# Delta-rule attention and two MoE layers on one core: the first MoE's weight words move to ScalarE's queue, with new priorities for keys and inverses

## The chip, the core and the metric

The kernel runs on one core of a Trainium2 chip. The metric is the device time of one execution in microseconds; the time given is the median of several executions. The core's engines are TensorE (PE in the rows), VectorE (DVE), ScalarE (ACT), GpSimd (POOL) and SyncE (SP). SP only issues DMAs here; ScalarE computes and issues some DMAs as well, in the order in which its instructions stand. A queue of DMAs is named after the engine that issues them (SPq, ACTq).

## The reference

Three layers follow one another; inputs are random, and the arithmetic of the kernel is in float32, with operands split in a high and a low part where TensorE works on them.

```python
# 1. delta-rule attention: 4 x 8 sequences, 768 steps, head size 48
k_n = k / (norm(k) + 1e-6)
for t in range(768):
    y[t] = q[t] @ state
    v_old = k_n[t] @ state
    state = state + beta[t] * outer(k_n[t], v[t] - v_old)
# 2. first MoE: x = y as (3072, 384)
h = x @ w_in                      # w_in (384, 2048), stored as float64
x = (h * sigmoid(h)) @ w_out      # w_out (2048, 384), stored as float64
# 3. second MoE: 8 experts, gate normalised by rows and columns 8 times
out = sum(P[:, e:e+1] * (relu(x @ w1[e]) @ w2[e]) for e in range(8))
```

## The kernel before

**Attention in chunks.** The 768 steps are cut into 12 chunks of 64, which the program calls steps s, and the 32 sequences into two groups bp = 0, 1. For each chunk the recurrence turns into matrix products once a 64 x 64 triangular system is inverted. For two chunks at a time, `tri(j)` inverts the diagonal 32 x 32 blocks of chunks 2j and 2j+1 of all sequences on VectorE: a start (line 538), 62 dependent operations, one column after the other (lines 546 and 548), and an end (line 561) that gives `tu`. ScalarE copies `tu` to `nu` in another order (line 564), SP writes both to memory (`rd`, line 569; `td`, line 578) and loads them back in the layout in which TensorE needs them (`rt`, line 588; `td11`, lines 593 and 596). `merge(s)` makes the off-diagonal block with TensorE (`z`, line 607; `r`, line 620), and the products `c`, `d`, `y`, `s`, `t` follow.

What an inverse needs are the key Grams of its two chunks. For chunks 2 and up, `keys(s, prio)` loads the keys (`ke`, line 354, by SP), makes two Gram tiles for each group on TensorE (`gkq`, lines 398 and 399), copies them from PSUM on ScalarE (line 414), and stores them by SP (`nd`, line 408; `gd`, line 404). There are 40 such tiles. `units(j)` reads `nd` back as `nu` (line 432). The roots that scale an inverse are taken on ScalarE for the first two (line 474) and on GpSimd for the others.

**The first MoE** runs while attention goes on: six batches b of 512 tokens, each ready when two chunks are done. For each of 16 blocks f of the hidden dimension TensorE makes `h` (nine products of 128 x 512, line 733) and `x2p` (nine, line 774). Between the two ScalarE takes the Sigmoid (line 739), VectorE multiplies (line 743), ScalarE rounds to the high part (line 747) and GpSimd makes the low part (line 751).

**Its weights** arrive as 64-bit words. `weight(kind, f, m)` loads one or two blocks (`wr`, line 861; 768 KB for two) and converts them: ScalarE takes the absolute value of the high words (line 865), VectorE runs seven operations (lines 886 to 897), ScalarE writes the high part (line 883). There are 20 such conversions, 12 of them pairs; n counts single blocks, 0 to 31. The words of pair n take the place of an earlier one, so their load waits until the absolute value of an earlier block is taken (`free`).

**The second MoE** starts at about 760 us in the profile, and takes the rest of the time.

**The order** is written by a list scheduler, the class `Order`. Each operation is added with an engine, a cost, what it depends on and a priority; the scheduler keeps a clock of each engine, and of the operations that could start first it takes the one with the highest priority. The result is a fixed order on each engine. SP alone is modelled as a queue of DMAs, with 8 in flight; a DMA on ScalarE is an operation of ScalarE with its issue as cost, and what waits for it is given a latency by hand. The names in the order below carry the step, the group and a running number: `gkq4_1_0` is the Gram 0 of step 4, group 1.

Of the kernel before, what the change touches and what calls it, by code (L numbers as in the profile page):

```python
# [12 lines left out]
I32 = mybir.dt.int32  # L13
# [188 lines left out]
def kernel(  # L202
# [14 lines left out]
    nc = tc.nc  # L217
# [10 lines left out]
    def f32(ap):  # L228
        return ap.bitcast(F32)
# [3 lines left out]
    def place(p, i=None, shape=(3072,), dtype=F32R, name=None):  # L233

        tag = f"w{p}" if i is None else f"w{p}_{i}"
        return persist.tile([128, *shape], dtype, tag=tag, name=name or tag)
# [55 lines left out]
    op = sc.add  # L292
    T = {}
    O = {}
# [8 lines left out]
    for i in range(4):  # L303
# [3 lines left out]
        out=nident, in0=tmpu[:, 0:128], in1=tmpu[:, 0:128], op=ALU.add), [(x, 0.13)], prio=40)  # L307
# [20 lines left out]
    def load_part(s, bp, part, prio):  # L328

        t = kplace(s, bp)  # L330
        a, b = slice(64, 112), slice(0, 48)
        after = [(x, -1.0) for x in O["nl", 0]] + [O["z", 2 * s + bp]] if part else []
        if s and not part:

            return [(op("ACT", 0.45, adma(t(a, 0), kq[s, bp, 0, :, 0]), prio=prio), 2.3),
                    (op("ACT", 0.45, adma(t(b, 0), kq[s, bp, 1, :, 0]), prio=prio), 2.3)]
        return [op("SP", 0.27, dma(t(a, part), kq[s, bp, 0, :, part]), after, prio=prio),
                op("SP", 0.27, dma(t(b, 2 * part), kq[s, bp, 1, :, part]), after, prio=prio)]
# [10 lines left out]
    def load_k(s, bp, prio):  # L349
        def go(ab):  # L350
            if ab == 0:
                T["ke", s, bp] = two.tile([128, 2, H, CH], F32, tag="ke", name=f"ke{s}_{bp}")
            o = 64 * (1 - ab)
            nc.sync.dma_start(out=T["ke", s, bp][o:o + 48], in_=kq[s, bp, ab])
        x = op("SP", 0.5, lambda: go(0), [(y, -1.0) for y in O["nl", 0]], prio=prio, take=["ke"])
        return [x, op("SP", 0.5, lambda: go(1), [(x, -9.0)], prio=prio)]
# [483 lines left out]
    def weight(kind, f, m):  # L840

        src, n = (w_out if kind else w_in), 4 * (f // 2) + 2 * kind + f % 2
        key = ("wr", n)
# [6 lines left out]
        p, i = n // 4, n % 4  # L850

        def ld():
            if p < NP - 2:
                if i == 0:
                    T["pw", p] = place(p + 1, shape=(4 * DM, 2), dtype=I32, name=f"wr{p}")
                T[key] = T["pw", p][:, DM * i:DM * (i + m)]
            elif n < 2 * NF - 1:
                T[key] = place(NP - 1, i + (p == NP - 1), (DM, 2), I32, f"wr{n}")
            else:
                T[key] = moe.tile([128, DM, 2], I32, tag="wx", bufs=1, name=f"wr{n}")  # L860
            nc.sync.dma_start(out=T[key], in_=src[:, f:f + m].bitcast(I32).rearrange("p f (c w) -> p (f c) w", w=2))

        def absolute():
            T["wt", n] = moe.tile([128, 2 * DM], F32, tag="stg", bufs=3, name=f"wt{n}")
# [32 lines left out]
            (1, lambda: v.scalar_tensor_tensor(out=part(1), in0=view(lw().bitcast(U32)), scalar=2.0 ** -43, in1=view(f32(hw())),  # L897
                                               op0=ALU.mult, op1=ALU.mult)),
        ]
        free = [O["wabs", n - 4 + j] for j in range(m)] if n >= 4 else []  # L900
        if n >= 4:
            free = free + [(x, -1.0) for x in O["nl", 0]]
        if 2 * NF - 4 <= n < 2 * NF - 1:
            free = free + [O["wlo", n - 3]]
        a = op("SP", 1.09 * m, ld, free, prio=-9 if n >= 4 else 9.2)
        first = op("ACT", 0.1 + 0.35 * m, absolute, [a] + ([O["wabs", n - 1]] if m == 1 and n else []), prio=-4, take=["stg"])

        if p == NP - 1:
            before = [O["wlo", n - 1 if i else n - 4]]
# [5 lines left out]
        for k, (two_, fn) in enumerate(ops):  # L915
            c = 0.09 + 0.47 * m if two_ else 0.13 + 0.22 * m
# [10 lines left out]
    def keys(s, prio):  # L927
        for bp in range(2):
            O["ke", s, bp] = load_k(s, bp, prio) if s >= 2 else load_part(s, bp, 0, prio)
            (gram_kq if s >= 2 else gram_k)(s, bp)  # L930
# [11 lines left out]
    for s in range(2):  # L942
# [5 lines left out]
        out=wgr[:, :, 1], in0=wgs, in1=f32(wgr)[:, :, 0], op=ALU.subtract), [x], prio=0)  # L948
    for p in range(NP):
        for kind in range(2):  # L950
            for f in range(2 * p, 2 * p + 2, 2 if p < NP - 2 else 1):
                weight(kind, f, 2 if p < NP - 2 else 1)
# [4 lines left out]
    for s in range(NSTEP):  # L957
        if s % 2 == 0 and s + 2 < NSTEP:
            if s:
                keys(s + 2, 6)  # L960
                keys(s + 3, 6)
            units(s // 2 + 1)
            tri(s // 2 + 1, 1.5 if s else 1.6)
        O["rtl", s], O["gll", s], O["tdl", s] = rt_load(s)
        merge(s)
        for bp in range(2):
            if s:
                state_read(s, bp)
            update(s, bp)
            output(s, bp)  # L970
            turn(s, bp)
            k = 2 * s + bp
            k = k + 4 if k < 3 else k + 3 if k > 3 else 2 * NSTEP
            if k < 2 * NSTEP:
                O.setdefault(("ld", k // 2), {})[k % 2] = load(k // 2, k % 2, -2.5)
                mask_q(k // 2, k % 2)
        if s + 2 < NSTEP:
            O["kv", s + 2] = load_kv(s + 2, -3.5)
            norms(s + 2)
        if s % 2:  # L980
            for f in range(NF):
                moe_h(s // 2, f)
                moe_o(s // 2, f)
# [458 lines left out]
```

## Time and profile before

| | us |
|---|---|
| median of 3 executions | 2282.77 (2282.16 to 2282.86) |
| profiled execution | 2280.6 |
| its span, first to last instruction | 2278.8 |
| TensorE busy | 2187.4 (96%) |
| VectorE busy | 1768.9 (78%) |
| GpSimd busy | 1552.9 (68%) |
| ScalarE busy | 1018.5 (45%) |
| mean granted TensorE clock | 0.973 of full speed |

The profile comes from one execution. The chain of work that ended last runs 61% of the span on TensorE, 15% on VectorE, 11% on GpSimd and 5% through DMAs. These are shares over the whole span; the stages differ, and the rows further down are read by stage.

### The profile page before, as it was taken

Reading aid. Unit: us, or ns where it says so; the run is one execution under the profiler, and the core shown is the slowest. Engines: PE = TensorE matmul, PEld = TensorE weight load, DVE = VectorE, ACT = ScalarE, POOL = GpSimd, SP = SyncE. Lnnn points to the kernel's source line nnn. Section 1 sums busy time; section 2 is a strip of 40 time slices with the busy share of each in tenths; the row PEclk is TensorE's granted clock in tenths of the full one; section 3 lists DMA queues with packets and bytes.
Section 4 is the critical chain, followed back from the end, with each engine's and each line's share of the span. In section 5 each row is a group of like instructions: output and inputs, shape, how many; then the busy total and the mean of one; then the engine's idle time right before and its main releaser. Section 6 shows DMA issues by size and latency. Waiting matters only on the chain.

```text
span 2278.8 us, 40177 instructions
## 1 busy us (share of the span) xinstructions
PE 2187.4 (96%) x15662; PEld 1918.5 (84%) x15662; DVE 1768.9 (78%) x2999; ACT 1018.5 (45%) x1766; POOL 1552.9 (68%) x1387
## 2 busy tenths in 40 slices
PE   7789998999999899999999999989999999999999
PEld 7677776788787789999898999978999999999998
DVE  6788776623825688888888888897888888888887
ACT  2344333333344446454444544446444454545453
POOL 0225165344428678888788888877878888888884
PEclk8689999999999999999999999999999999999999
DMA  8764534432120200101111111111111111110101
GB/s 244 183 144 129 144 76 91 104 75 66 36 65 34 84 28 28 42 29 38 33 35 35 35 35 30 41 46 39 36 35 36 35 35 36 35 35 28 43 28 49
DMA packets 127421, 136.76 MB, mean 60 GB/s; under 512 B 83392, under 2 KB 91328, under 8 KB 127232
## 3 DMA queue, kind: packets, MB, share of 16 engines
q1 hardware_dynamic: 124864, 133.55, 21.6%
q8 instruction: 123, 2.02, 0.4%
q10 hardware_dynamic: 2368, 0.66, 0.2%
q14 instruction: 66, 0.54, 0.1%
HBM read 108.47 MB, written 25.69 MB: 59 GB/s over the span
## 4 chain that ended last, share of the span: by engine, by line
PE 61%; DVE 15%; POOL 11%; DMA 5%; issue 3%; ACT 2%; SPq 2%; POOLq 0%; DVEq 0%; ACTq 0%
PE o L1291 29%; PE p L1204 23%; PE x2p L774 3%; DVE s L1014 3%; POOL room L1014 2%; DVE tu L546 2%; PE h L733 2%; DVE tmpu L548 2%; POOL wa L1014 2%; POOL wraw L1014 2%; POOL g L751 1%; POOL h L1014 1%; DMA ke<-in_kq 1%; DVE sg L743 1%; POOL du L524 1%
## 5 line engine op out<-in xcount | busy, mean ns | idle before, releaser
L1204 PE MATMUL p<-room,wa 128*128 128x512 f32 x2880 | 738.0, 397 | 5.5 <-DVE s L1014 5.5
L1204 PEld LDWEIGHTS p<-room,wa 128*128 128x128 f32 x2880 | 537.7, 189 | 104.2 <-issue 5.9
L1291 PE MATMUL o<-wb,room 128*128 128x384 f32 x2784 | 603.9, 339 | 2.9 <-POOL room L1014 0.9
L1014 DVE TENSOR_TENSOR s<-s,p 128x512 f32<-128x512 f32 x704 | 476.2, 684 | 161.4 <-ACT s L1218 77.5
L1291 PEld LDWEIGHTS o<-wb,room 128*128 128x128 f32 x2784 | 499.8, 189 | 25.5 <-DVE acc L1307 6.5
L1014 POOL TENSOR_TENSOR room<-s,room 128x512 fp32r<-128x512 f32 x232 | 317.7, 1370 | 235.3 <-ACT s L1237 134.3
L1307 DVE SCALAR_TENSOR_TENSOR acc<-o,pr,acc 128x384 f32<-128x384 f32 x708 | 418.6, 612 | 34.2 <-PE o L1291 32.7
L1291 PE MATMUL o<-wb,h 128*128 128x384 f32 x1824 | 420.0, 338 | 3.1 <-DVE acc L1014 1.6
L1291 PEld LDWEIGHTS o<-wb,h 128*128 128x128 f32 x1824 | 329.6, 188 | 22.7 <-issue 2.2
L1014 POOL TENSOR_TENSOR wa<-wraw,wa 128x640 fp32r<-128x640 f32 x189 | 323.5, 1724 | 1.7 <-ACT wa L1107 1.7
L1235 ACT ACTIVATE room<-s 128x512 fp32r<-128x512 f32 x232 | 145.6, 628 | 387.8 <-DVE s L1014 387.8
L751 POOL TENSOR_TENSOR g<-sg,g 128x512 fp32r<-128x512 f32 x96 | 131.1, 1367 | 239.6 <-ACT g L747 239.2
L1014 POOL TENSOR_TENSOR wraw<-wraw 128x256 f32<-128x256 f32 x378 | 274.8, 748 | 13.9 <-DMA wraw<-in_w 4.2
L1237 ACT ACTIVATE s<-s 128x512 f32<-128x512 f32 x384 | 243.1, 633 | 12.2
L774 PE MATMUL x2p<-g,w 128*128 128x512 f32 x864 | 229.7, 409 | 18.5 <-POOL g L751 14.1
L1107 ACT ACTIVATE wa<-wraw 128x640 fp32r<-128x640 f32 x189 | 138.4, 732 | 234.8 <-POOL wraw L1014 218.3
L733 PE MATMUL h<-x,w 128*128 128x512 f32 x864 | 224.1, 409 | 3.1 <-ACT x L709 0.9
L1014 DVE TENSOR_TENSOR s<-p,s 128x512 f32<-128x512 f32 x320 | 219.1, 685 | 6.0 <-PE p L1204 1.8
L1014 POOL TENSOR_TENSOR h<-s,h 128x512 fp32r<-128x512 f32 x152 | 210.9, 1388 | 9.5 <-ACT s L1237 9.5
L774 PEld LDWEIGHTS x2p<-g,w 128*128 128x128 f32 x864 | 159.7, 192 | 63.3 <-POOL g L751 22.8
L1014 DVE TENSOR_TENSOR s<-s,s 128x512 f32<-128x512 f32 x192 | 210.8, 1098 | 2.3
L733 PEld LDWEIGHTS h<-x,w 128*128 128x128 f32 x864 | 164.7, 195 | 40.1 <-DVE sg L743 1.4
(177 smaller groups left out, 2246.6 us busy)
## 6 DMA issues: line engine op xcount, KB each, us to landing
wraw<-in_w SPq DMA_DIRECT2D x126, 384.0 KB, 3.0
kv<-in_kv SPq DMA_DIRECT2D x12, 768.0 KB, 4.9
ke<-in_kq SPq DMA_DIRECT2D x40, 192.0 KB, 3.6
kqp<-in_kq SPq DMA_DIRECT2D x40, 192.0 KB, 4.1
nd<-ke SPq DMA_DIRECT2D x20, 256.0 KB, 2.1
gd<-ke SPq DMA_DIRECT2D x20, 256.0 KB, 3.7
kqp<-gd SPq DMA_DIRECT2D x40, 128.0 KB, 4.0
wr<-in_w_in SPq DMA_DIRECT2D x6, 768.0 KB, 6.5
```

What stands on the lines that cost most here:

```text
L546: nc.vector.tensor_tensor(out=tu[:, a:b, 0:k], in0=tu[:, a:b, 0:k], in1=tv, op=ALU.add)
L548: nc.vector.tensor_tensor(out=tv, in0=nu[:, a:b, t:k].to_broadcast([128, b - a, k]), in1=tu[:, t:k, 0:k].to_broadcast([128, b - a, k]), op ...
L733: nc.tensor.matmul(out=ps.rearrange("p (s t) -> p s t", s=2), lhsT=w[:, k, wl], rhs=X1[:, at, k, xl], start=n == 0, stop=n == 8)
L751: nc.gpsimd.tensor_tensor(out=g[:, 1], in0=T["sg", b, f], in1=f32(g)[:, 0], op=ALU.subtract)
L774: nc.tensor.matmul(out=T["x2p", b][j], lhsT=w[:, wl, 128 * j:128 * j + 128], rhs=g[:, gl], start=f == 0 and n == 0, stop=f == NF - 1 and n ...
L1014: e.tensor_tensor(out=out, in0=in0, in1=in1, op=o)
L1107: nc.scalar.activation(P2[key][:, :, 0], R(3 + 5 * g, 8 + 5 * g), AF.Copy)
L1204: nc.tensor.matmul(out=ps, lhsT=w[:, i, wl], rhs=x[:, xl], start=k == 0, stop=k == 2)
L1235: nc.scalar.activation(P2[key][:, 0], buf(x), AF.Relu)
L1237: op2("ACT", 0.52, lambda: nc.scalar.activation(buf(x), buf(x), AF.Relu), writes=[("s", n, x)], prio=PR_H)
L1291: nc.tensor.matmul(out=ps, lhsT=h[:, hl, 128 * i:128 * i + 128], rhs=w[:, wl], start=c == 0, stop=c == 5)
L1307: op2("DVE", 0.53, lambda A=A, pk=pk, t=t: nc.vector.scalar_tensor_tensor(out=A(), in0=P2[pk], scalar=P2["pr"][:, t, e:e + 1], in1=A(), op ...
```

## The change

It moves the load of the words of the first MoE's weights from SP to ScalarE (line 861). In the scheduler's terms that operation is now one of ScalarE with 0.45 us, and the absolute value waits 2.5 + 2.5 m us behind it. The load of block n waits for the absolute value of block n − 8 instead of n − 4. The priority of these loads is −3 instead of −9. The keys of steps 4 and up get −12 instead of 6, and the inverses from the third on 1.2 instead of 1.5.

```diff
-            nc.sync.dma_start(out=T[key], in_=src[:, f:f + m].bitcast(I32).rearrange("p f (c w) -> p (f c) w", w=2))
+            nc.scalar.dma_start(out=T[key], in_=src[:, f:f + m].bitcast(I32).rearrange("p f (c w) -> p (f c) w", w=2))
...
-        free = [O["wabs", n - 4 + j] for j in range(m)] if n >= 4 else []
+        free = [O["wabs", n - 8 + j] for j in range(m)] if n >= 8 else []
...
-        a = op("SP", 1.09 * m, ld, free, prio=-9 if n >= 4 else 9.2)
-        first = op("ACT", 0.1 + 0.35 * m, absolute, [a] + ([O["wabs", n - 1]] if m == 1 and n else []), prio=-4, take=["stg"])
+        a = op("ACT", 0.45, ld, free, prio=-3 if n >= 4 else 9.2)
+        first = op("ACT", 0.1 + 0.35 * m, absolute, [(a, 2.5 + 2.5 * m)] + ([O["wabs", n - 1]] if m == 1 and n else []), prio=-4, take=["stg"])
...
             if s:
-                keys(s + 2, 6)
-                keys(s + 3, 6)
+                keys(s + 2, -12)
+                keys(s + 3, -12)
             units(s // 2 + 1)
-            tri(s // 2 + 1, 1.5 if s else 1.6)
+            tri(s // 2 + 1, 1.2 if s else 1.6)
```

The order that the scheduler writes differs from there on in many places. Three of them follow.

ScalarE ahead of the square root of the first inverse (line 474), before the change; what stands in brackets is what the instruction waits for, DMAHW and a number being one of the eight semaphores that DMAs share in turn:

```order
L883 ACTIVATE w_229<-wt_198 128x6x128 [waits DVE_49]
L432 DMA nu<-nd_224 16x32x32 [waits DMAHW5_49,DMAHW0_49]
L432 DMA nu<-nd_224 16x32x32 [waits DMAHW2_49]
L883 ACTIVATE w_229<-wt_221 128x2x384 [waits DVE_49]
L474 ACTIVATE du<-rta 128x32 [waits DVE_49]
```

The same place with the change:

```order
L432 DMA nu<-nd_220 16x32x32 [waits DMAHW5_49,DMAHW0_49]
L432 DMA nu<-nd_220 16x32x32 [waits DMAHW2_49]
L883 ACTIVATE w_276<-wt_231 128x6x128 [waits DVE_49]
L861 DMA wr_289<-in_w_in 128x1536 [waits DMAHW4_49]
L861 DMA wr_289<-in_w_out 128x1536 [waits DMAHW7_49]
L861 DMA wr_304<-in_w_in 128x1536 [waits DMAHW1_49]
L861 DMA wr_304<-in_w_out 128x1536 [waits DMAHW4_49]
L474 ACTIVATE du<-rta 128x32 [waits DVE_49]
```

Four loads of words now stand between the loads of `nu` and the root, and the last of them waits for semaphore 4, which the first of them was given.

ScalarE around the copy of the first inverse (line 564), before:

```order
L414 ACTIVATE ke3_0_472<-gkq3_0_1_597 128x512
L414 ACTIVATE ke3_0_472<-gkq3_0_0_621 128x512
L865 ACTIVATE wt8_668<-wr2_572 128x768
L414 ACTIVATE ke3_1_556<-gkq3_1_1_646 128x512
L414 ACTIVATE ke3_1_556<-gkq3_1_0_674 128x512
L564 ACTIVATE nu_94<-tu_95 128x32x32
L414 ACTIVATE ke4_0_723<-gkq4_0_1_778 128x512
```

and with the change:

```order
L414 ACTIVATE ke3_0_466<-gkq3_0_1_529 128x512
L414 ACTIVATE ke3_0_466<-gkq3_0_0_552 128x512
L414 ACTIVATE ke3_1_522<-gkq3_1_1_577 128x512
L414 ACTIVATE ke3_1_522<-gkq3_1_0_604 128x512
L414 ACTIVATE ke4_0_635<-gkq4_0_1_662 128x512
L414 ACTIVATE ke4_0_635<-gkq4_0_0_691 128x512
L414 ACTIVATE ke4_1_683<-gkq4_1_1_721 128x512
L564 ACTIVATE nu_94<-tu_95 128x32x32
L414 ACTIVATE ke4_1_683<-gkq4_1_0_751 128x512
```

Three Gram copies of step 4 (`ke4_0`, `ke4_1`) that came behind the copy to `nu` now come ahead of it, and the absolute values of line 865 are gone from this stretch.

ScalarE where Grams of steps 10 and 11 are copied: before, they stand in the middle of the third batch of the MoE (`sg2_12` is the Sigmoid of batch 2, block 12), behind the `z` of step 8:

```order
L414 ACTIVATE ke10_1_3340<-gkq10_1_1_5449 128x512
L739 ACTIVATE sg2_12_5511<-h2_12_5484 128x512
L747 ACTIVATE g2_12_5523<-sg2_12_5511 128x512
L414 ACTIVATE ke10_1_3340<-gkq10_1_0_5494 128x512
L739 ACTIVATE sg2_13_5555<-h2_13_5528 128x512
L747 ACTIVATE g2_13_5571<-sg2_13_5555 128x512
L414 ACTIVATE ke11_0_3587<-gkq11_0_1_5538 128x512
L739 ACTIVATE sg2_14_5607<-h2_14_5578 128x512
L747 ACTIVATE g2_14_5619<-sg2_14_5607 128x512
L414 ACTIVATE ke11_0_3587<-gkq11_0_0_5590 128x512
```

With the change, the last of the 40 Gram copies stands in the second batch, right ahead of the copy of `z` of step 6 (`zt6`):

```order
L564 ACTIVATE nu_94<-tu_95 128x32x32
L678 ACTIVATE y5_1_4278<-y5_1_4238 128x384
L739 ACTIVATE sg1_12_4315<-h1_12_4281 128x512
L747 ACTIVATE g1_12_4334<-sg1_12_4315 128x512
L739 ACTIVATE sg1_13_4353<-h1_13_4321 128x512
L747 ACTIVATE g1_13_4359<-sg1_13_4353 128x512
L739 ACTIVATE sg1_14_4379<-h1_14_4341 128x512
L414 ACTIVATE ke11_1_3137<-gkq11_1_0_4361 128x512
L613 ACTIVATE zt6_4431<-z6_4385 32x512 x2
```

So the Gram tiles that were spread to the third batch and beyond lie ahead of step 6.

## Rows read from the trace of the kernel before

**Rows 1.** Windows: length, busy time of each engine, clock, DMA share, GB/s.

```profile
0.00:126.00 126.00, 96.25 (x1712) 90.64 (x1712) 92.62 (x269) 40.43 (x71) 18.53 (x27) 0.74 0.81 209
126.00:256.00 130.00, 117.03 (x1510) 91.46 (x1510) 113.98 (x215) 57.49 (x99) 48.41 (x42) 0.93 0.56 135
...
760.00:2279.00 1519.00, 1496.89 (x7502) 1353.39 (x7502) 1299.46 (x2035) 738.85 (x1258) 1240.98 (x1090) 0.99 0.12 38
```

**Rows 2.** Tile `wr` (words): ns min/median/max, starts; last, landing.

```profile
L889 DVE SCALAR_TENSOR_TENSOR wt<-wr,wt x20: 551/951/2014, 12.3 to 250.6; 128x768 int32<-128x768 int32 x12, 128x384 int32<-128x384 int32 x8
L891 DVE TENSOR_SCALAR wr<-wr x20: 350/544/1181, 13.7 to 251.1; 128x768 int32<-128x768 int32 x12, 128x384 int32<-128x384 int32 x8
L893 DVE SCALAR_TENSOR_TENSOR wr<-wr x20: 546/952/1074, 14.3 to 251.7; 128x768 int32<-128x768 int32 x12, 128x384 int32<-128x384 int32 x8
L895 DVE TENSOR_SCALAR wr<-wt x20: 349/552/565, 15.3 to 252.3; 128x768 int32<-128x768 int32 x12, 128x384 int32<-128x384 int32 x8
L897 DVE SCALAR_TENSOR_TENSOR w<-wr x20: 540/946/1464, 15.9 to 253.3; 128x768 fp32r<-128x768 uint32 x12, 128x384 fp32r<-128x384 uint32 x8
...
DMA to landing us min/median/max: 3.3/5.5/10.9
```

**Rows 3.** SP's timeline, 20 to 66 us: start, duration, line, operation.

```profile
33.74 0.45 SPq L861 DMA_DIRECT2D wr<-in_w_in  x1
...
35.58 7.29 SPq L354 DMA_DIRECT2D ke<-in_kq  x4
...
54.65 5.71 SPq L354 DMA_DIRECT2D ke<-in_kq  x4
...
61.95 0.50 SPq L569 DMA_DIRECT2D rd<-nu  x1
```

**Rows 4.** The chain of waits to 60 us: issue, us to landing.

```profile
4.03 6.08 DMA wr<-in_w_in
...
16.48 3.36 DMA nd<-gneg
...
35.94 11.47 DMA ke<-in_kq
```

**Rows 5.** ScalarE's timeline to 130 us; in brackets idle time and its releaser.

```profile
24.55 0.23 ACT L474 ACTIVATE du<-rta 128x32 f32<-128x32 f32 x1 [2.83 <-DVE rta L472]
...
54.06 1.95 ACT L564 ACTIVATE nu<-tu 128x1024 f32<-128x1024 f32 x1
```

**Rows 6.** VectorE: ends of inverses 1 and 3, two multiplies of the MoE.

```profile
48.83 1.23 DVE L561 TENSOR_TENSOR tu<-tu,du 128x1024 f32<-128x1024 f32 x1
...
172.15 0.69 DVE L743 TENSOR_TENSOR sg<-h,sg 128x512 f32<-128x512 f32 x1 [5.18 <-ACT sg L739]
...
241.18 0.69 DVE L743 TENSOR_TENSOR sg<-h,sg 128x512 f32<-128x512 f32 x1 [4.07 <-ACT sg L739]
...
273.37 1.23 DVE L561 TENSOR_TENSOR tu<-tu,du 128x1024 f32<-128x1024 f32 x1
```

**Rows 7.** TensorE's timeline, 125 to 438 us: rows with waits.

```profile
125.80 0.51 PE L733 MATMUL h<-x,w 128*128 128x512 f32 x1 [0.93 <-ACT x L709]
...
224.61 2.14 PE L774 MATMUL x2p<-g,w 128*128 128x512 f32 x8 [1.20 <-DVE w L897]
...
234.67 0.29 PE L398 MATMUL gkq<-ke 48*64 48x64 f32 x2 [2.39 <-DMA ke<-in_kq]
...
358.67 1.72 PE L607 MATMUL z<-rt,td 32*32 32x32 f32 x64 [4.52 <-DMA rt<-rd]
...
437.38 0.22 PE L607 MATMUL z<-rt,td 32*32 32x32 f32 x2 [1.03 <-DMA rt<-rd]
```

**Rows 8.** Windows, tile `gkq` (key Grams) alone, 438 to 625 us.

```profile
438.00:625.00 187.00, 6.89 (x192) 6.06 (x192) 3.50 (x6) 1.00 0.27 67
```

**Rows 9.** Windows, 590 to 626 us, all engines.

```profile
590.00:626.00 36.00, 31.04 (x186) 23.21 (x185) 26.44 (x53) 10.29 (x15) 9.59 (x7) 1.00 0.19 38
```

**Rows 10.** Windows, 20 to 50 us, all engines.

```profile
20.00:50.00 30.00, 22.55 (x290) 21.79 (x290) 25.44 (x131) 6.58 (x11) 0.00 (x0) 0.81 1.00 277
```

## The prediction, made before the changed kernel was run

> **What bounds the kernel now.** I read the windows view first, by stage. After 760 us TensorE is busy 1496.89 of 1519 us [rows 1]: the second MoE is bound by TensorE's work, and the change moves nothing there. What can move is the time at which that stage begins. Before it TensorE is idle for 126 − 96.25 = 29.75 us up to the first product of the first MoE (`h`, at 125.80) and for 13 us in the 130 us after that [rows 1, 7].
>
> The second view was what releases the first stage. On the chain of waits the words of the first weights take 6.08 us from issue to landing, and a load of keys issued at 35.94 takes 11.47 us [rows 4]. SP's own rows say why: words issued at 33.74 (and more of them right behind) stand in the same queue ahead of these keys, and SP's group of four key loads lasts 7.29 us, a later one 5.71 us; only behind that can SP issue `rd`, at 61.95 [rows 3]. `rd` is the inverse on its way to memory. The inverse itself ended at 48.83 + 1.23 = 50.06 on VectorE [rows 6], and its copy on ScalarE ran at 54.06 for 1.95 [rows 5].
>
> The third view was TensorE's waits later on: 4.52 us for `z` at 358.67 and 1.03 at 437.38, both for `rt`, that is, for an inverse [rows 7]. So from 125 to 440 us the chain of inverses (`tri`) on VectorE sets the end, and work that TensorE could do beside it only fills waits.
>
> "Measurable" means here more than 0.2%, 4.6 us. The sum is made against the profiled execution (2280.6 us; 2278.8 of span, 1.8 around it) and laid on the median, 2282.77, 2.2 above it.
>
> **The change part by part.** *Words to ScalarE's queue, first stage.* SP loses 20 issues of words, 0.45 us for the one shown [rows 3], and the words that lie in its queue ahead of keys; keys come sooner. Against that, ScalarE now issues words in order with its computing. Ahead of the square root of the first inverse stand four loads of words, and the last waits for the semaphore that the first of them was given, so the root cannot start before that load has landed. Ahead of this group ScalarE has loads of `nu` that need `nd`, and `nd` landed at 16.48 + 3.36 = 19.8 [rows 4]; 6.08 us later [rows 4] is 25.9, against 24.55 for the root before [rows 5]: the root comes some 1.4 us late, unless `nd` comes sooner with no words ahead of it. Next, the copy of the inverse (`nu`, line 564) now stands behind three more Gram copies, which need keys of step 4; before, they came behind it. I expect the copy at 59 to 61 instead of 54.06. But SP issued `rd` at 61.95 only, so most of that delay has cover: SP, which was blocked until then, is free now. If that cover is gone, the delay counts in full. Term: **+1.0**. Bounds: below, `rd` could go right behind the inverse and its copy, 50.06 + 1.95 = 52.0, not 61.95: −9.9. Above, words land after 10.9 us at worst [rows 2]; twice 10.9 − 6.1 is +9.6. I take a value near the middle since both waits are visible and both have cover.
>
> *Eight tiles ahead, and the inverses against the conversion.* Of the conversion five instructions fewer stand ahead of the first multiply of the MoE on VectorE (one each of lines 889, 891, 893, 895, 897): medians 0.95 + 0.54 + 0.95 + 0.55 + 0.95 = 3.9 us [rows 2] that are left for later. Two multiplies of 0.69 us fewer [rows 6] stand ahead of the end of the third inverse: −1.4. VectorE stood idle for 5.18 and 4.07 us, waiting for a Sigmoid [rows 6]; words that are there eight tiles ahead give it conversions for that time. None of the 9.25 is the one bound, all of it the other; I take half, −4.6, since the order has to offer the work at that very place. End of the third inverse (273.37 + 1.23 before [rows 6]): 1.0 + 3.9 − 1.4 − 4.6 = **−1.1**. With the bounds of the first term: −16.7 to +12.1. TensorE's waits upstream of it, 1.20 for a converted weight and 2.39 for keys [rows 7], get shorter or longer with no effect of their own, because the wait for `z` takes up the difference.
>
> *Keys of later steps "last".* The new priority, −12, doesn't put them last: at the place where `z6` stands in the order all 40 Gram tiles of steps 2 to 11 lie ahead, against 34 before. Six Gram tiles are 6.89 us of TensorE [rows 8]. In their place two `x2p` tiles fewer (of nine products; eight took 2.14 us [rows 7], so 2.4) lie ahead of `z6`; ahead of `z8` one `h` and one `x2p` fewer. So 6.9 − 4.8 = 2.1 us more of work fits ahead of a moment that the inverses set: **−2.1**. Bounds: 0, and both waits, 4.52 + 1.03 = −5.6. The load of these keys on SP costs nothing new, since the count is the same and SP has lost 20 loads of words.
>
> *Fifth inverse earlier.* With the Grams of steps 10 and 11 done, the last inverse can run behind the one before it instead of at 600 us. In 590 to 626 us TensorE is busy 31.04 of 36 [rows 9]: 5.0 idle, as VectorE has the inverse and the MoE's multiplies at once. I take half, **−2.5** (bounds −5.0 and 0): the multiplies and the copies of `g` wait for one another anyhow.
>
> *Inverse's priority 1.2 for 1.5:* conversions go first while there are any; that is in the −1.1 already.
>
> Sum: −1.1 − 2.1 − 2.5 = −5.7. 2282.77 − 5.7 = **2277.1 us**. The bounds add up to −27 and +12.
>
> **A rule that speaks against it.** In 20 to 50 us the DMA engines' share is 1.00 at 277 GB/s [rows 10]: they were full, whoever issued. The Trainium skill, "DMA: Bandwidth & Descriptors", section "Issuing engines are not separate DMA queues", says that transfers of all issuing engines run on the same 16 DMA engines and that issuing from several saves only the sequencer's time. By that the first term would be no gain at all; it is the second rival. The same page, section "Queues, rings and completion order", has each DMA engine take turns between the queues that have work, packet by packet; by this the keys would no longer stand behind whole loads of words, and 11.47 would come nearer to what a load takes alone. No row here shows two busy queues side by side, so the sum leans on neither.
>
> **The rivals.** *Slower: ScalarE is held at semaphores.* ScalarE makes the Sigmoids, the Gram copies and the copy of the inverse; a load of words that waits for its turn holds all of that. Price: the first stage +9.6 (two waits for words that land at 10.9), and in the MoE none of VectorE's idle time filled, since the Sigmoids that it waits for stand behind words: 9.6 + 3.9 − 1.4 = +12.1, with the two other terms 12.1 − 2.1 − 2.5 = +7.5: **2290.3**. It decides from the point where the first copy of `nu` starts later than about 66 us, or the idle time before line 743 grows. For it: the order has that wait ahead of the root. Against it: ScalarE was busy 40.43 of 126 us [rows 1], and words land at 5.5 us in the median [rows 2].
>
> *No change: the transfers were the limit.* Start as before, idle time not filled, fifth inverse without effect: 0 + 3.9 − 1.4 − 2.1 = +0.4: **2283.2**. For it: the share of 1.00. Against it: SP's blocked stretches are there in the rows. In this case the words on another queue do not do what the change says, and the keys, as shown, don't in any.
>
> *Larger gain: SP's freedom carries through.* The 5.71 us in which SP was held at key loads [rows 3] come off the first stage instead of +1.0: 2277.1 − 6.7 = **2270.4**. Against it: the copy of `nu` stands behind Grams of step 4 in the order.
>
> **How the numbers follow.** Forecast 0.46, of which 0.33 lies beyond the measurable; its own range is 2272 to 2282. Slower rival 0.24 (0.22 beyond, 0.02 within), no change 0.17 (0.13 within, 0.04 slower, as its own start may slip), larger gain 0.13. Faster 0.33 + 0.13 = 0.46, same 0.13 + 0.02 + 0.13 = 0.28, slower 0.22 + 0.04 = 0.26. The range, 2267 to 2291, takes in all four centres; the full sum of the bounds, −27 to +12, is cut below, as it needs every one at its best.
>
> **What would show it.** Right: first `h` at 125 to 128; the copy of `nu` at 58 to 62 with `rd` right behind it; the end of the third inverse at 272 to 275; the wait before `z6` under 2.5 us; the fifth inverse ended before 560; the whole gain there before 760 us, and the rest of the kernel as long as before. Wrong: the first `h` beyond 133, or idle time before line 743 that grows (ScalarE held); the end of the third inverse later than 277; or a first `h` before 121 (larger gain).

## The result, and the profile after

The changed kernel takes **2307.36 us** (median of 4 executions, 2299.19 to 2308.91), the kernel before 2282.47 beside it: the ratio is 1.0115, with a 95% interval of 1.0095 to 1.0134. It is slower by about 25 us; faster was forecast, by 5.7. The profiled execution is the quickest of the four (2299.19, span 2297.0), so its profile accounts for 18.2 us over the span of before. The second MoE starts 23 us late in it and is then some 5 us shorter than in the profile of before; over the profiles of all runs its length varies by more than that, from 1518.5 to 1527.1 us, so I take the 23 us as what the first stages lose.

Windows of the changed kernel, same columns as [rows 1]:

```profile
0.00:126.00 126.00, 81.85 (x1471) 77.28 (x1471) 70.69 (x233) 34.62 (x61) 15.93 (x25) 0.69 0.79 199
126.00:256.00 130.00, 111.52 (x1539) 90.08 (x1540) 120.27 (x219) 58.08 (x97) 49.93 (x43) 0.90 0.56 141
...
760.00:2297.00 1537.00, 1516.23 (x7603) 1373.74 (x7601) 1299.27 (x2048) 750.24 (x1276) 1251.27 (x1100) 0.99 0.12 37
```

In the first 126 us TensorE does 81.85 us of work instead of 96.25 [rows 1]. The last stage is still TensorE's own: 1516.23 of 1537. The granted clock is lower in the first two stages (0.69 and 0.90, against 0.74 and 0.93 [rows 1]), but the products of the first MoE are no slower for it: by the profile pages one of `h` takes 402 ns in the mean (409 before), one of `x2p` 413 (409). So the loss arises early, and I follow it by the rows that answer to [rows 7]. TensorE's timeline, changed kernel: the first `h`, then `z` of steps 6, 8 and 10, then the first product of the second MoE.

```profile
142.60 0.50 PE L733 MATMUL h<-x,w 128*128 128x512 f32 x1
...
384.95 2.11 PE L607 MATMUL z<-rt,td 32*32 32x32 f32 x64 [5.66 <-DMA rt<-rd]
...
464.19 0.22 PE L607 MATMUL z<-rt,td 32*32 32x32 f32 x2 [2.64 <-issue]
...
571.80 1.20 PE L607 MATMUL z<-rt,td 32*32 32x32 f32 x64
...
777.42 1.80 PE L1204 MATMUL p<-room,wa 128*128 128x512 f32 x7
```

The last two of these points in the kernel before:

```profile
624.40 0.24 PE L607 MATMUL z<-rt,td 32*32 32x32 f32 x2 [0.70 <-DMA rt<-rd]
...
754.27 2.02 PE L1204 MATMUL p<-room,wa 128*128 128x512 f32 x8
```

| | before | after | shift |
|---|---|---|---|
| first `h` | 125.80 [rows 7] | 142.60 | +16.8 |
| end of the third inverse (start + duration) | 274.60 [rows 6] | 298.07 | +23.5 |
| `z` of step 6 | 358.67 [rows 7] | 384.95 | +26.3 |
| `z` of step 8 | 437.38 [rows 7] | 464.19 | +26.8 |
| `z` of step 10 | 624.40 | 571.80 | −52.6 |
| first product of the second MoE | 754.27 | 777.42 | +23.1 |

`z` of step 10 comes earlier, as the last inverse does; since the second MoE does not, other work that stood ahead of it now stands behind it. Some two thirds are lost ahead of the first `h`. ScalarE's timeline there (issues of words on its queue, the root, the last Gram copy and the copy of the first inverse); it answers to [rows 5]:

```profile
20.32 0.47 ACTq L861 DMA_DIRECT2D wr<-in_w_in  x1
...
22.19 0.33 ACTq L861 DMA_DIRECT2D wr<-in_w_in  x1
27.59 0.33 ACTq L861 DMA_DIRECT2D wr<-in_w_out  x1
27.97 0.23 ACT L474 ACTIVATE du<-rta 128x32 f32<-128x32 f32 x1 [6.83 <-DMA wr<-in_w_in]
...
72.56 0.60 ACT L414 ACTIVATE ke<-gkq 128x512 f32<-128x512 f32 x1 [2.20 <-PE gkq L399]
73.05 1.95 ACT L564 ACTIVATE nu<-tu 128x1024 f32<-128x1024 f32 x1
```

The root starts at 27.97 instead of 24.55: the fourth load of words was issued at 27.59, right before it, as the order had said. The copy of the inverse starts at **73.05** instead of 54.06, right behind a Gram copy of step 4. The inverse itself had ended 3.3 us later than before (53.4 against 50.06). So the copy waited some 20 us behind copies of Gram tiles that it does not need; the last copy of step 3, which stood ahead of it before as well, was at 60.14, so step 4 makes about 12 of them.

Why those were late is in the chain of waits up to the first `h` (issue, us to landing), which answers to [rows 4]:

```profile
20.82 11.97 DMA wr<-in_w_out
...
33.21 9.59 DMA kv<-in_kv
42.81 6.29 DMA gd<-ke
49.17 4.19 DMA ke<-in_kq
...
63.03 3.52 DMA nd<-ke
...
66.99 3.48 DMA ke<-in_kq
...
75.82 3.07 DMA rd<-nu
```

Words issued at 20.82 land at 32.79. SP, whose next DMAs take their semaphores in turn with ScalarE's, can go on only then: the load of `kv` is issued at 33.21, and it delays the store `gd` (42.81). That store frees the buffer for the keys of step 3 (49.17, against 35.58 in [rows 3]); their stores free that for the keys of step 4 (66.99), whose Grams stand ahead of the copy, and `rd` follows at 75.82 instead of 61.95. SP's timeline shows the standing:

```profile
24.43 8.74 SPq L298 DMA_DIRECT2D kqp<-in_kq  x4
...
37.18 1.12 SPq L298 DMA_DIRECT2D kqp<-in_kq  x2
40.03 0.78 SPq L298 DMA_DIRECT2D kq<-in_kq  x2
...
49.17 4.54 SPq L354 DMA_DIRECT2D ke<-in_kq  x4
```

Four loads of queries take 8.74 us. The next goes at 37.18, when the words of 22.19 have landed; tile `wr` has the longest time to landing in the view:

```profile
DMA to landing us min/median/max: 3.3/5.8/15.0
```

22.19 + 15.0 = 37.2. Before, the longest was 10.9 [rows 2].

The DMA engines were full here as before: the window that answers to [rows 10], and from the DMA view of 28 to 36 us the two queues with their packets, MB and share of the 16 engines' time. q10 is ScalarE's (13.24 MB in the whole kernel, 0.66 before), q1 is SP's:

```profile
20.00:50.00 30.00, 13.99 (x174) 13.34 (x174) 22.02 (x118) 5.98 (x10) 0.00 (x0) 0.64 1.02 300
```

```profile
q10 hardware_dynamic: 288, 1.58, 71.7%
q1 hardware_dynamic: 284, 0.62, 30.5%
```

The two queues moved equally many packets, and those of the words were larger. So the words had 72% of the engines' time, and the keys, queries and stores 30%. Nor were the words used any earlier for it. Those of 20.32, landed by 27.6, had their conversion ended (line 897) at 117.2 us, those of 33.74 in the kernel before at 79.3; on VectorE both conversions stand behind a wait for a product `gq` of TensorE, and this wait was nearly twice as long. VectorE's rows, changed kernel and kernel before:

```profile
75.92 2.85 DVE L455 TENSOR_TENSOR kqp<-gq,mask 64x512 f32<-64x512 f32 x4 [20.09 <-PE gq L452]
...
116.27 0.94 DVE L897 SCALAR_TENSOR_TENSOR w<-wr 128x768 fp32r<-128x768 uint32 x1
```

```profile
62.48 2.85 DVE L455 TENSOR_TENSOR kqp<-gq,mask 64x512 f32<-64x512 f32 x4 [10.56 <-PE gq L452]
...
77.80 1.46 DVE L897 SCALAR_TENSOR_TENSOR w<-wr 128x768 fp32r<-128x768 uint32 x1
```

The other third lies between the first `h` and the end of the third inverse. VectorE's windows from the first `h` to that end, changed kernel and kernel before (columns as in [rows 1]; VectorE is the third):

```profile
142.60:298.10 155.50, 137.25 (x1805) 110.08 (x1802) 137.47 (x264) 67.67 (x119) 58.00 (x50) 0.95 0.51 138
```

```profile
126.00:274.60 148.60, 135.43 (x1698) 106.10 (x1697) 131.50 (x254) 64.35 (x112) 53.25 (x47) 0.94 0.56 137
```

VectorE has 137.47 us of work there instead of 131.50, and is idle for 18.0 instead of 17.1 us. The extra work is conversions: by its groups in these windows lines 886 to 897 took 73.7 us instead of 64.0, while the multiplies of line 743 fell from 21 to 19. Its rows, which answer to [rows 6], show the waits for a Sigmoid little changed (5.07 and 3.54, against 5.18 and 4.07), the late third inverse, and the last one, `tri(5)`, whose last operation now starts at 529.61 (before it ended at 615.8). The prediction and the expectations call this one the fifth, by its index:

```profile
190.01 0.69 DVE L743 TENSOR_TENSOR sg<-h,sg 128x512 f32<-128x512 f32 x1 [5.07 <-ACT sg L739]
...
260.71 0.69 DVE L743 TENSOR_TENSOR sg<-h,sg 128x512 f32<-128x512 f32 x1 [3.54 <-ACT sg L739]
...
296.84 1.23 DVE L561 TENSOR_TENSOR tu<-tu,du 128x1024 f32<-128x1024 f32 x1
...
529.61 2.25 DVE L561 TENSOR_TENSOR tu<-tu,du 128x1024 f32<-128x1024 f32 x1
```

### The profile page after: what moved, and what is told of

The parts are those of the page before. It is cut to its first block, busy times and chain, and to the rows that moved or that the text cites. A ratio compares the mean times of both kernels' runs of the same rounds, so it can differ in the third digit from the quotient of the medians.

```text
span 2297.0 us, 40042 instructions
## 1 busy us (share of the span) xinstructions
PE 2179.3 (95%) x15588; PEld 1918.1 (84%) x15588; DVE 1761.7 (77%) x2999; ACT 1023.6 (45%) x1766; POOL 1554.7 (68%) x1387
## 3 DMA queue, kind: packets, MB, share of 16 engines
q10 hardware_dynamic: 5248, 13.24, 2.0%
## 4 chain that ended last, share of the span: by engine, by line
PE 67%; DVE 12%; POOL 8%; DMA 6%; issue 4%; SPq 1%; ACT 1%; ACTq 0%; DVEq 0%; POOLq 0%
PE o L1291 31%; PE p L1204 25%; PE x2p L774 4%; PE h L733 4%; DVE tu L546 2%; DVE tmpu L548 2%; POOL wa L1014 2%; POOL wraw L1014 1%; DVE s L1014 1%; POOL room L1014 1%; POOL g L751 1%; DMA wr<-in_w_out 1%; DMA kv<-in_kv 1%; POOL du L524 1%; POOL h L1014 1%
## 5 line engine op out<-in xcount | busy, mean ns | idle before, releaser
L1014 DVE TENSOR_TENSOR s<-s,s 128x512 f32<-128x512 f32 x192 | 199.0, 1036 | 2.4
```

The source lines that it names most:

```text
L1014: e.tensor_tensor(out=out, in0=in0, in1=in1, op=o)
```

## The experiments

Medians are in us; kernels that ran together share their runs of the kernel before (2279.9 to 2280.5). A 95% interval of the ratio to it stands in brackets.

**Parts alone.** First the queue: line 861 alone, so that the order is word for word that of before.

```diff
-            nc.sync.dma_start(out=T[key], in_=src[:, f:f + m]...
+            nc.scalar.dma_start(out=T[key], in_=src[:, f:f + m]...
```

> Only line 861: the words go to ScalarE's queue at the places in the order where SP issued them; lookahead, priorities and the scheduler's view of them are those of before. Theory A (the copy of the first inverse stands behind Gram copies of step 4, whose keys come late because the DMA engines are full; the order is at fault): the order of that copy is that of before, so it starts between 52 and 60 us, and the time is 2275 to 2290. Theory B (ScalarE is held at semaphores by words, wherever its copies stand): two loads of words stand ahead of the first root and seven ahead of the copy, so the copy starts after 64 and the time is above 2293.

Measured: 2291.71 (1.0049 [1.003, 1.0068]). The copy starts at 58.5, as A said and not as B did, but the time is between the two. SP's row of two `gd` stores, and the first `h`:

```profile
32.41 7.52 SPq L404 DMA_DIRECT2D gd<-ke  x2
```

```profile
132.75 0.50 PE L733 MATMUL h<-x,w 128*128 128x512 f32 x1
```

The second store went at 39.61, when words that ScalarE had issued at 33.77 landed (39.54): 7.52 us for two stores. The first `h` is 7.0 us late. VectorE also has a new wait behind it, for a product `c`:

```profile
195.37 0.56 DVE L644 TENSOR_TENSOR wq<-kv,c 128x384 f32<-128x384 f32 x1 [8.07 <-PE c L640]
```

Then the other two parts: lookahead eight with the words on SP, and the priorities of keys and inverses together.

```diff
-        free = [O["wabs", n - 4 + j] for j in range(m)] if n >= 4 else []
+        free = [O["wabs", n - 8 + j] for j in range(m)] if n >= 8 else []
```

> Only the lookahead of eight tiles, with words on SP as before. Theory A: nine loads of words instead of seven stand ahead of the store of the first inverse in SP's queue, keys of step 4 behind it; some loss, 2284 to 2294. Theory C (the lookahead alone makes the loss, by words that fill the DMA engines in the first 50 us): 2298 or more.

Measured: 2286.17 (1.0026 [1.001, 1.0041]), a small loss, as A said; C falls.

```diff
-                keys(s + 2, 6)
-                keys(s + 3, 6)
+                keys(s + 2, -12)
+                keys(s + 3, -12)
...
-            tri(s // 2 + 1, 1.5 if s else 1.6)
+            tri(s // 2 + 1, 1.2 if s else 1.6)
```

> Only the priorities of the keys (-12) and of the inverses (1.2); words as before. Theories A, B and C: the first inverse and the first product of the first MoE stay where they were (126 us, within 1), and the time is 2274 to 2283. Theory D (the keys' priority makes the loss): 2290 or more.

Measured: 2281.15 (1.0008 [0.9992, 1.0024]); D falls, and no gain can be told either. Each of the two alone, in five rounds:

> The kernel before with the inverses' priority of 1.2 alone. Theories G and I: conversions go ahead of the third inverse, which ends 0 to 3 us earlier or later; 2277 to 2284, no difference that can be told.

> The kernel before with the keys' priority of -12 alone. Theories G and I: the Grams of steps 10 and 11 come early and the fifth inverse 60 to 80 us earlier; 2276 to 2284. If the gain that was forecast for the fifth inverse is there by itself, below 2279.

Measured: 2279.23 (0.9999 [0.999, 1.0008]) and 2281.69 (1.0001 [0.9988, 1.0014]). With the keys' priority alone the last inverse ends some 73 us earlier than before (541.50 + 1.23 against 615.8), and the time does not follow:

```profile
541.50 1.23 DVE L561 TENSOR_TENSOR tu<-tu,du 128x1024 f32<-128x1024 f32 x1
```

TensorE's rows of that run, `z` of steps 6 and 8 and the first product of the second MoE:

```profile
359.36 1.85 PE L607 MATMUL z<-rt,td 32*32 32x32 f32 x52 [4.51 <-DMA rt<-rd]
...
446.29 1.20 PE L607 MATMUL z<-rt,td 32*32 32x32 f32 x64
...
756.77 1.56 PE L1204 MATMUL p<-room,wa 128*128 128x512 f32 x6
```

The Grams put ahead of step 6 did not fill the wait there (4.51 us, 4.52 before); `z` of step 8 comes 8.9 us later than before, and of these all but 2.5 are back at the second MoE. Work was moved ahead, not into a gap.

**The copy, the words, the lookahead in the changed kernel.** First the copy ahead of the Gram copies of steps 4 and later:

```diff
-        r = op("ACT", 1.0, lambda: ...
+        O["nuc", j] = r = op("ACT", 1.0, lambda: ...
...
-                   m[k:] + ([(q, 0.0)] if k == 0 else []), prio=4.5)
+                   m[k:] + ([(q, 0.0)] if k == 0 else []) + ([(O["nuc", 0], 0.0)] if s >= 4 else []), prio=4.5)
```

> The changed kernel, with the Gram copies of step 4 and later held behind the copy of the first inverse. Theory A: the copy starts at about 61 us, behind the Gram copies of step 3 alone, instead of 73; the first product of the MoE comes at 129 to 133 instead of 142.6, and the time is 2290 to 2298. Theory B: ScalarE is held as before, the copy starts after 68, the time stays above 2302.

Measured: 2299.03 (1.009 [1.0061, 1.0119]). The copy is where A put it, the rest is not: `rd` goes only at 69.15, since on SP it stands behind keys of step 4 as well. ScalarE's and SP's rows:

```profile
59.72 1.94 ACT L564 ACTIVATE nu<-tu 128x1024 f32<-128x1024 f32 x1
```

```profile
69.15 0.50 SPq L569 DMA_DIRECT2D rd<-nu  x1
```

The order of one engine, mended alone, moves the wait to the next. The first `h` came at 140.3.

Words of tiles 4 to 11 at an eighth of their bytes, in the changed kernel (GpSimd fills the rest of the buffer with zeros, so these weights are not the reference's):

```diff
-            nc.scalar.dma_start(out=T[key], in_=src...)
+            c = DM * m // 8 if 4 <= n < 12 else DM * m; c < DM * m and nc.gpsimd.memset(T[key][:, c:DM * m], 0)
+            nc.scalar.dma_start(out=T[key][:, 0:c], in_=src...[:, 0:c])
```

> The changed kernel, but the four loads of words of tiles 4 to 11 bring an eighth of their bytes; GpSimd, idle there, fills the rest of the buffer with zeros, so those weights are not the reference's. Order and number of DMAs stay. Theory F (the loss is in the transfer of these words: they fill the DMA engines, and SP, which takes its semaphores in turn with ScalarE, stands until they have landed): SP's loads of queries and keys no longer stand for them, the keys of step 3 are issued by 40 us instead of 49.2, the copy of the first inverse starts before 64, the first product of the MoE comes before 132, and the time is 2282 to 2292. Theory A (the order of the copies alone): the copy starts after 68, time above 2298.

Measured: 2303.68 (1.01 [1.0085, 1.0115]), as A said; but the copy came at 66.2 and the first `h` at 137.3, between the two. The tiles behind were still whole, and SP stood for those. So the same for tiles 4 to 23:

> As the run with small words, but for tiles 4 to 23: an eighth of the bytes, the rest zeros by GpSimd, those weights not the reference's. Theory F (transfers of words in the first stage, through full DMA engines and shared semaphores): the store of the gd tile no longer waits to 39.2, the first product of the MoE comes at 126 to 133 instead of 142.6 (137.3 with tiles 4 to 11 alone). Theory G: it comes at 134 to 138, since the order of copies and the keys' buffers still set it. Of the time both say 2295 to 2304, because the MoE's own loss, from 160 to 300 us, was there with small words as well.

Measured: 2293.69 (1.0061 [1.0046, 1.0077]). The first `h` is where F put it, 11.2 us earlier than in the changed kernel and 5.6 later than before:

```profile
131.44 0.50 PE L733 MATMUL h<-x,w 128*128 128x512 f32 x1
```

The time is below what both theories said, and the copy still came late, at 65.1. Of the 16.8 us some 11 are therefore the words' transfers, in an order that is written as if they took none. Two edits that only thin the words out early were misses. All words from tile 4 held behind the copy (one dependence more on `free`):

> The changed kernel, with all words from tile 4 on held behind the copy of the first inverse. Theory F: without them in the first 50 us the keys of step 3 are issued by 38, the copy (still behind eleven Gram copies) starts at 56 to 63; the conversions come later, which costs VectorE some of what it has to spare; time 2283 to 2296. Theory A: the copy starts after 66, the time is 2298 or more.

Measured: 2306.58 (1.0117 [1.0102, 1.0132]). The copy comes at 61.4 and the first `h` at 135.6, but the second inverse ends at 179.9, against 168.3 in the changed kernel, and the third at 297.2, hardly earlier than there (298.1): the gain is lost again. And a lookahead of four in the changed kernel:

> The changed kernel with a lookahead of four tiles again: four instead of six loads of words ahead of the first root, six instead of eight ahead of the copy. Theory F: the words in the first 40 us are half as many, the copy starts at 60 to 67, time 2288 to 2300. Theory A: the order of copies is the same, copy after 68, time 2300 or more.

Measured: 2312.5 (1.0137 [1.0122, 1.0152]), the copy at 71.3. F, as the whole cause, falls.

**Order against queue.** The changed order with line 861 on SP's queue, at the places where ScalarE has it:

> The changed kernel's order on every engine, but line 861 issues on SP's queue at the places where ScalarE has it. Theory G (the order is the larger part: the scheduler no longer counts the words in SP's queue, so keys, Grams and copies stand at places for which their transfers are late): time 2293 to 2306, the copy of the first inverse after 64 us. Theory H (the queue of ScalarE is the larger part; its loads make SP and ScalarE stand for one another's semaphores): time 2278 to 2290, the copy before 62.

Measured: 2308.88 (1.0119 [1.0102, 1.0137]), somewhat above what G said and far above H. ScalarE's copy of the first inverse:

```profile
77.71 1.95 ACT L564 ACTIVATE nu<-tu 128x1024 f32<-128x1024 f32 x1
```

It is later than with the words on ScalarE's queue. On GpSimd's queue, in the order of before and in the changed order (line 861 with `nc.gpsimd`):

> The kernel before with line 861 on GpSimd's queue, whose DMAs take other semaphores than those that SP and ScalarE share; the places in the order are those of before. Theory F: SP no longer waits for words through its semaphores, nor does ScalarE stand; the store of the gd tile that waited from 32.8 to 39.6 us in the run with the queue alone goes at 33 to 35, and the time is 2274 to 2284. Theory B (whatever computing engine issues words is held): GpSimd's low parts in the MoE come late, the time is 2288 or more.

> The changed kernel's order, words issued on GpSimd's queue, with other semaphores than SP's and ScalarE's. Theory G: the order alone still costs 10 or more, 2290 to 2302. Theory H: near the time of the words on GpSimd in the old order, 2282 to 2290.

Measured: 2286.61 (1.0028 [1.0015, 1.0041]), between the two, and 2301.69 (1.0083 [1.0059, 1.0107]), as G said. The order is the same here, but not the times: GpSimd had issued seven loads of words by 8.7 us in the one run and eight by 9.0 in the other, and all of them had landed by 28.3. Together:

| words issued by | order of before | changed order |
|---|---|---|
| SP | 2280.3 | 2308.9 |
| ScalarE | 2291.7 | 2307.4 |
| GpSimd | 2286.6 | 2301.7 |

The order costs 15 to 29 us whichever engine issues; the queue, in the changed order, next to nothing or a gain. H falls. What makes the order is shown by the words on ScalarE's queue and in its model (with the new priority of the loads, −3), lookahead, keys and inverses as before:

> The words on ScalarE's queue and counted by the scheduler as ScalarE's, at lookahead four, with the old priorities of keys and inverses. Theory G: the order changes as in the changed kernel, eleven Gram copies ahead of the copy of the first inverse; 2300 to 2314. Theory H: no slower than the queue alone, 2286 to 2296.

Measured: 2305.18 (1.0117 [1.0096, 1.0138]), the copy at 72.3. Against the queue alone (2291.7) only the scheduler's view of the words is new, their priority included, and the loss is nearly whole.

**The transfers counted.** The changed kernel, whose scheduler again counts each load of words in its one queue of transfers:

```diff
-                        lane = lanes[-8] + 0.1 if e in self.QUEUES and len(lanes) >= 8 else 0.0
-                        c.append((max(r, now[e], lane), i))
+                        lane = lanes[-8] + 0.1 if len(lanes) >= 8 else 0.0
+                        c.append((max(r, now[e], lane if e in self.QUEUES or self.ops[i][7] < 0 else 0.0), i))
...
-                    now[e] = end[i] = t + cost
+                    now[e], queue = t + cost, max(t + 1.1, queue) - 1.09 * cols if cols < 0 else queue; end[i] = queue if cols < 0 else now[e]; cols < 0 and lanes.append(queue)
...
-        a = op("ACT", 0.45, ld, free, prio=-3 if n >= 4 else 9.2)
-        first = op("ACT", 0.1 + 0.35 * m, absolute, [(a, 2.5 + 2.5 * m)] + ...
+        a = op("ACT", 0.45, ld, free, prio=-3 if n >= 4 else 9.2, cols=-m)
+        first = op("ACT", 0.1 + 0.35 * m, absolute, [(a, 0.93)] + ...
```

> The changed kernel, but the scheduler counts a load of words on ScalarE's queue as it counts one of SP's: its 1.09 us per block go into the one queue of transfers, it waits for the eighth DMA before it, and the absolute value waits for that transfer's end. The order then has five Gram copies ahead of the copy of the first inverse instead of eleven. Theory G (the order is wrong because these transfers are missing from the scheduler's queue): that copy starts before 62 us, the first product of the MoE comes at 125 to 134, and the time is 2280 to 2294. Rival I (what costs is conversions and Grams put off into the MoE, whatever the first stage does): the first product comes earlier, but the time stays above 2297.

Measured: **2283.2** (1.0015 [1.0006, 1.0025]): by the ratios 26 us of loss become 3.4, with the words still on ScalarE's queue, eight ahead, and the new priorities. The copy and the first `h`:

```profile
59.97 1.97 ACT L564 ACTIVATE nu<-tu 128x1024 f32<-128x1024 f32 x1
```

```profile
127.27 3.08 PE L733 MATMUL h<-x,w 128*128 128x512 f32 x11
```

G holds for the changed kernel, and I falls. It does not say all about the order, though. With the transfers counted, lookahead four and all old priorities:

> As the run with the transfers counted, but with lookahead four and all old priorities: against the run with the queue alone only the scheduler's view of the eight shared semaphores and of ScalarE's issue differs. Theory G: 2282 to 2293, no slower than the queue alone (2291.7). Rival I: as fast as the queue alone, since nothing is put off.

Measured: 2301.42 (1.0088 [1.0069, 1.0107]), a miss for both. The old priorities of keys and inverses, and the old lookahead, each by itself:

> The run with the transfers counted (2283.2), with the old priorities of keys and inverses and the lookahead of eight kept. If the old priorities are what made the run with lookahead four and old priorities slow (2301.4, lost from 450 us on), this one is at 2292 or more, and the keys' -12 belongs to the words on ScalarE's queue. If the lookahead of four made it, this one is at 2280 to 2288. Theory G alone says only that the first product of the MoE stays within 125 to 132.

> The run with the transfers counted, with lookahead four and the new priorities kept. If lookahead four is what costs, 2290 or more; if the old priorities are, 2280 to 2288. Theory G alone: first product at 125 to 132.

Measured: 2303.86 (1.0105 [1.0083, 1.0128]) and 2297.3 (1.0076 [1.006, 1.0093]). In all three the first `h` comes at 125.9 to 131.1 and the third inverse ends at 276.6 to 280.5; so the first stages are mended. In the orders that do not count the transfers (the changed kernel and the runs with lookahead four, on SP, on GpSimd, and with queue and model alone) the first `h` comes at 139.6 to 146.0 and that inverse ends at 298.1 to 307.2. Either old value costs by itself. The three lose their time after 280 us, in the way that rival I told. With the old keys the last inverse is late again:

```profile
641.50 1.22 DVE L561 TENSOR_TENSOR tu<-tu,du 128x1024 f32<-128x1024 f32 x1
```

What in the order after 280 us makes these three slow is open, and so it may be luck that the run with 2283.2 is spared it: that counting the transfers mends the stages up to the third inverse is shown in all four orders, that nearly the whole loss goes with it in one of them. No version beat the kernel before by more than its noise.

## Why the prediction was wrong

**Words to ScalarE's queue, first stage (+1.0; measured +16.8): the step that failed.** The root behind the words was right in kind, and cost 3.4 instead of 1.4: the words took 27.59 − 20.32 = 7.3 us, not 6.08, were issued 0.5 us later than assumed, and the fourth issue itself took another 0.4. Right too was the place: the copy behind Gram copies of step 4. What failed is the estimate of 59 to 61 for the copy and the cover for it: the copy came 19.0 us later, and `rd` still 13.9. The estimate took for granted that keys would come sooner with the words out of SP's queue. The keys of step 3 came later, at 49.17 instead of 35.58: SP stood for the words through the shared semaphores, the engines were as full as [rows 10] had shown (1.02, at 300 GB/s), and while both queues had work the words took 72% of their time. The upper bound, +9.6, was too low, since it multiplied one landing time by two, and three stages of keys and stores lay behind one another.

**Third inverse (−1.1, that is −2.1 beyond the first term; measured +6.7 beyond it).** I took half of VectorE's idle time as filled. None was: 17.1 us became 18.0. The work put behind the first multiply was +6.0 us by the windows, not 3.9 − 1.4 = 2.5; the −1.4 is there (19 multiplies instead of 21), what was too small is the term of the conversions. They were held ahead of the first `h`, where VectorE stood for `gq`: it did 86.9 us of work up to there, 92.4 before. My reading, which no run tests alone, is that words that lie ready do not fill a wait for a Sigmoid unless the order has conversions at that place.

**Keys (−2.1; measured +2.8 from the third inverse to `z` of step 6).** The order did change as told, all 40 Grams ahead. The wait before `z` grew, to 5.66 from 4.52. TensorE, 23 us late by then, waited for the inverse all the same. The keys' priority alone shows the step without the rest: the wait before `z` of step 6 stayed at 4.51, and step 8 came 8.9 us later, so the work did not fit into the waits.

**Last inverse, called the fifth (−2.5; measured 23.1 − 26.8 = −3.7 in the changed kernel).** The size is near, but it is not shown that the inverse makes it: the Grams that moved ahead are missing from the same stretch. As a gain it did not show: with the keys' priority alone that inverse ends 73 us earlier, and the time is the same.

**The rule.** [rows 10] has the engines full, and the Trainium skill, "DMA: Bandwidth & Descriptors", section "Issuing engines are not separate DMA queues", says that another issuing engine saves the issue alone. The runs agree in the changed order, where it mattered little which engine issued (2301.7 to 2308.9); in the order of before it mattered more (2280.3 to 2291.7), and there the trace shows a wait at a shared semaphore (7.52 us for two stores, above). I gave it the part of a rival without loss, and missed what follows from it here: if the transfers still run on the same engines, then the change's edit of the scheduler's costs, 2.18 us of queue for a pair turned into 0.45 us of ScalarE, is wrong, and every place in the order that rests on SP's queue being free is too early. That was in the diff. The section "Queues, rings and completion order" of that page of the Trainium skill has each DMA engine take turns between the queues, packet by packet. The trace agrees: 288 packets of one queue beside 284 of the other. That did not shelter the keys: a load of them issued at 24.08 beside the words took 8.9 us to land, against 5.9 at most for the same four before.

**The slower rival** had its point of decision passed (66 us; 73.05 measured) and its price, 2290.3, was 17 short. Its mechanism was not the main one: words on ScalarE's queue cost 11 us in the old order, where the wait shown above is SP's, and in the changed order the loss is there with ScalarE issuing no words.

The signs that I named did their work: the first `h` beyond 133 and the third inverse later than 277 were both there.

## What to carry to other kernels

Where an order comes from a scheduler's model, a transfer that is moved to another queue must stay in the model's bandwidth. Left out, it cost 13 us here (with the loads' new priority); put back, it gave 24 us in the changed kernel, 15 with lookahead four (2312.5 to 2297.3), and hardly more than the noise with all old priorities (2305.2 to 2301.4). A model that is right about one resource does not make a list scheduler's order good everywhere. Before such a change is priced, look for instructions that overtake one another on an in-order engine, and ask when what now stands ahead is ready by the trace, not by the model. A queue that is relieved in the order gave nothing back here, where the engines behind it were full.

## What was not expected of the hardware

An issue on one engine stood until a transfer of another engine's queue had landed, as the two share eight semaphores in turn: in the changed kernel SP's load at 37.18 behind ScalarE's words of 22.19, with the words alone on ScalarE's queue SP's store at 39.61 behind those of 33.77. With the words on GpSimd's queue, whose DMAs use other semaphores, the same two stores took 1.79:

```profile
38.10 1.79 SPq L404 DMA_DIRECT2D gd<-ke  x2
```

That run is no test of the semaphores, though: all words issued by then had landed by 25.1 us, so no load of words was under way.

Two queues that both had work moved equally many packets, 288 and 284 in 8 us, and by the size of their packets 1.58 and 0.62 MB. So the queue with the larger packets had most of the engines' time.

The time to landing of words rose to 15.0 us, from 10.9 at most before, though in both kernels no more than three loads of words were under way at once.
